# Top-k attention with channel mix: the weighted sums move behind the scores in PSUM, the ranks behind the exponentials, weighing stands after turning, the 1e-9 is added early

## The chip, the cores and the metric

The kernel runs on one core of one Trainium2 chip. The metric is the device time of one execution in microseconds (us); lower is better.

## What is computed

```python
# attention: B, H, S, D = 8, 8, 576, 64; top_k = 32
scores = scale * np.matmul(q, k.transpose(0, 1, 3, 2))
kth = np.partition(scores, -top_k, axis=-1)[..., -top_k:-top_k + 1]
scores = np.where(scores >= kth, scores, -1000000000.0)
attn = np.exp(scores - np.max(scores, axis=-1, keepdims=True))
attn = attn / (np.sum(attn, axis=-1, keepdims=True) + 1e-09)
x = np.matmul(attn, v)            # then (B, S, H * D)
# channel mix: d_model 512, d_ff 1024
xk = mu_k * x + (1.0 - mu_k) * x_prev
xr = mu_r * x + (1.0 - mu_r) * x_prev
k = np.maximum(xk @ w_k, 0.0)
out = 1.0 / (1.0 + np.exp(-(xr @ w_r))) * (k * k @ w_v)
```

All of it is float32, at full precision.

## The kernel before

The attention is cut into 288 tiles of 128 query rows by 576 keys. A visit is one pair of heads (`hp`) of one batch with either four tiles (`i` = 0 to 3) or five (`i` = 4 to 8; tile 8 holds the last 64 rows of both heads). Four tiles, or tile 8 alone, make a unit: there are 96 of them. `pipeline` runs a software pipeline: each turn of its `while` loop is one slot `n`, in which every stage works on another tile. Tile n is scored (`scores`, L230 and L234, TensorE) and copied out (`keep`, L239, ScalarE); tile n-1 gives candidates (`candidates`, L263, VectorE); tile n-2 is ranked, bounded and counted (`bounds` L274, `count` L279 on ScalarE, `below` L282 on GpSimd); tile n-3 gets its threshold from nine ranks (`threshold`, L287), its exponentials (`exps`, L290, ScalarE) and its mask with the row sums (`mask`, L293, VectorE); tile n-4 is turned (`turn_tile`, four transposes L309, two more at L319 for the last 64 columns of a pair of tiles) and copied out by ScalarE (L310, L320); for tile n-5, if its number is odd or 8, a pair of tiles is weighed with the values (`weigh`, L367 and L369: 16 matmuls and 4, 160 times in all). Once for each unit ScalarE adds 1e-9 to the row sums (`inverse`, L325), VectorE takes the reciprocal (`inverse2`, L329), GpSimd spreads it (`spread`, L334), TensorE turns it (`turn_inverse`, L340), ScalarE copies it out (L345, L349), and VectorE multiplies it onto the weighted sums (`place`, L374 to L379).

The order of these steps inside a slot is the list `ORDER` (L42); each engine runs its own instructions strictly in that order. Between them the class `Lanes` puts the work of the channel mix: matmuls (`mix`, L427 to L429) at the end of TensorE's slot, copies out of PSUM at `evac` and other ScalarE work at `act`, as far as a budget of planned costs (`PACE`, `SHARE`, `PIECE`) allows. The budget and the costs are the same before and after, so the same matmuls stand in the same slots.

PSUM has eight banks of 512 float32 values per partition. Two banks hold one tile of scores, with the nine `ranks` in the same two banks. Two more hold the exponentials of one tile (576 values, so 64 of them lie in the second bank), and behind them the weighted `sums`. The other four go round (`psM`) for everything that is turned or mixed. There is one buffer each of scores and of exponentials, and instructions of different engines that touch the same bank wait for each other, reads included. So before the change the weighing waits for this slot's exponentials (both lie in the same bank) and the mask for the weighing; the scores wait for `nine` (L287) of the slot before, which reads the ranks, and `nine` waits for `keep`.

Of the kernel before, what the change touches and what calls it, by code (L numbers as in the profile page):

```python
# [9 lines left out]
F32 = mybir.dt.float32  # L10
# [3 lines left out]
AF = mybir.ActivationFunctionType  # L14
OP = mybir.AluOpType
PSUM = bass.MemoryType.PSUM

B, H, S, D = 8, 8, 576, 64
# [3 lines left out]
HS = S // 2  # L22
# [16 lines left out]
PACE, SHARE, PIECE, CAP, MOST = 4.60, 0.74, 1.52, 4.45, 2  # L39
END, HASTE = 36, 1.20  # L40
EXPS, EVAC = 3, (0, 'et')
ORDER = """exp score weigh turn prep inv loads evac keep best0 c0 drop0 c1 best1 c2 drop1 first c3 best2 c4 bounds eighth count norm et high below act late c5 norm2 early thr c6 second place mix mask dve pool weights""".split()  # L42


@with_exitstack
def topk_attention_channel_mix(ctx: ExitStack, tc: tile.TileContext, q, k, v, mu_k, mu_r, w_k, w_v, w_r, out):
    nc = tc.nc
# [25 lines left out]
    def open_pools(stack, g, sfx):  # L73
        p = lambda n, bufs, **kw: stack.enter_context(tc.tile_pool(name=n + sfx, bufs=bufs, **kw))
        g.one = p("one", 1)
        g.two = p("two", 2)
        g.three = p("three", 3)
        g.four = p("four", 4)

        scored = p("psS", 1, space=PSUM).tile([128, 2 * 512], F32, name="ps")  # L80
        g.ps, g.ranks = scored[:, 512 - HS:512 + HS], scored[:, :9]


        g.se = p("psE", 1, space=PSUM).tile([128, 2 * 512], F32, name="se")
        g.pe = g.se[:, :S]
        g.sums = g.se[:, S:S + 256], g.se[:, S + 256:S + 320]
        nc.vector.tensor_copy(g.ranks, ranks_i)
        g.turns = 0
        g.ready = range(3 * HP + NFB) if sfx else []
        g.psM = g.psT = p("psM", 4, space=PSUM)  # L90
# [134 lines left out]
    def scores(g, P, i):  # L225
        hs = [slice(e * 64, (e + 1) * 64) for e in range(2)]
        if i < 2 * NKC:
            c, j = divmod(i - P.first, 2)
            for e, h in enumerate(hs):
                nc.tensor.matmul(g.ps[:, e * HS:(e + 1) * HS], lhsT=P.qs[j][h, c * 128:(c + 1) * 128], rhs=P.K[h, j], start=True, stop=True)  # L230
        else:
            for j in range(2):
                for e, h in enumerate(hs):
                    nc.tensor.matmul(g.ps[hs[j], e * HS:(e + 1) * HS], lhsT=P.qr[h, hs[j]], rhs=P.K[h, j], start=True, stop=True)  # L234
        return g.ps

    def keep(g, T):
        T.sc = g.four.tile([128, S], F32, name="sc")
        nc.scalar.activation(T.sc, T.ps, AF.Copy)  # L239

    def pick_exact(g, T):
        top = g.four.tile([128, TOPK], F32, name="top")
# [109 lines left out]
    def weigh(g, U, u):  # L352
        P = U.P
        if u == 0:
            U.pa = g.sums[U.u // 2]
        hs = [slice(j * 64, (j + 1) * 64) for j in range(2)]
        if U.u < 2:
            pa = U.pa[:, u * 128:(u + 1) * 128]
            ms = [[U.et[u, j][:, c, :] for j in range(2)] for c in range(NKC)]
            ls = [U.el[u][:, j * 128:(j + 1) * 128] for j in range(2)]  # L360
        else:
            pa = U.pa
            ms = [[U.et[0, 0][:, c, h] for h in hs] for c in range(NKC)]
            ls = [U.el[0][:, h] for h in hs]
        for c in range(NKC):
            for j in range(2):
                nc.tensor.matmul(pa[hs[j]], lhsT=P.v[:, j, c, :], rhs=ms[c][j], start=(c == 0), stop=False)  # L367
        for j in range(2):
            nc.tensor.matmul(pa[hs[j]], lhsT=P.vr[:, j], rhs=ls[j], start=False, stop=True)  # L369

    def place(U):
        xT, hp = U.xT, U.P.hp
        if U.u < 2 and U.P.near:
            nc.vector.tensor_mul(xT[:, hp, 1 + U.u * 256:1 + (U.u + 1) * 256], U.pa, U.ri)  # L374
        elif U.u < 2:
            x = xT[:, hp, 1:1 + MAIN].rearrange("p (q c) -> p c q", c=NKC)[:, 2 * U.u:2 * U.u + 2, :]
            nc.vector.tensor_mul(x, U.pa.rearrange("p (c q) -> p c q", c=2), U.ri.rearrange("p (c q) -> p c q", c=2))
        else:
            nc.vector.tensor_mul(xT[:, hp, 1 + MAIN:], U.pa, U.ri[:, :64])  # L379

# [186 lines left out]
    class Lanes:  # L567
# [9 lines left out]
        def at(self, slots, place, f, lane=None, cost=0.0):  # L577
            item = Env()
            item.f, item.lane, item.cost, item.done = f, lane, cost, False
            self.todo.setdefault((self.slot + slots, place), []).append(item)  # L580
            return item
# [16 lines left out]
        def run(self, place):  # L598
            for item in self.todo.pop((self.slot, place), []):
                self.do(item)  # L600
            while (item := self.first(self.queue.get(place, []))) and self.free[place] >= item.cost * SHARE:
                self.do(item)
                self.queue[place].remove(item)
# [79 lines left out]
    def new_batch(g):  # L683
        x = g.two.tile([128, HP, 1 + S], F32, name="xT")
        nc.gpsimd.memset(x[:, :, 0:1], 0.0)
        return x

    def pipeline(g):
# [91 lines left out]
        while n < total + 7 or "next" in state or L.busy():  # L780
# [21 lines left out]
            def score():  # L802
                if n < total:
                    P = Ps[p]
                    T = tiles[n] = Tile_()
                    T.n, T.i, T.P = n, i, P
                    if i == P.first:
                        if p % HP == 0:
                            state["seen"] = g.two.tile([128, HP, 3, 9], F32, name="seen")
                        P.group, P.seen = state["seen"], state["seen"][:, p % HP]  # L810
                    if i % 4 == 0:
                        U = units[p, i // 4] = Env()
                        U.u, U.P = i // 4, P
                        U.rs = g.four.tile([128, 4], F32, name="rs")
                    T.U = units[p, i // 4]
                    T.rs = T.U.rs[:, i % 4:i % 4 + 1]
                    T.ps = scores(g, P, i)
                    L.use("pe", 0.5)
# [23 lines left out]
            def weigh_():  # L842
                if W and (W.i % 2 or W.i == 8):
                    weigh(g, W.U, W.i // 2 % 2)
                    L.use("pe", 1.33 if W.i % 2 else 0.7)
# [31 lines left out]
            def ranks_(f, r):  # L877
                if C:
                    f(C, r)
# [15 lines left out]
            def keep_():  # L895
                if n < total:
                    keep(g, tiles[n])
                    L.use("act", 0.53)
# [43 lines left out]
            do.update({f"drop{r}": lambda r=r: ranks_(drop, r) for r in range(2)})  # L942
            for step in ORDER:
                if step in do:
# [7 lines left out]
    with ExitStack() as stack:  # L952
        g = Env()
        open_pools(stack, g, "")
        stack.enter_context(tc.manual_schedule())
        pipeline(g)
# [12 lines left out]
    with tc.If(again > 0):  # L969
        with tc.For_i(0, B, 1) as b, ExitStack() as stack:  # L970
            g = Env()
            open_pools(stack, g, "_again")
            L = Direct()
            xT = new_batch(g)
            rows = out[bass.ds(b, 1)].rearrange("o s d -> (o s) d")
            for hp in range(HP):
                P = Env()
                P.hp = hp
                prep_all(g, P, lambda x: x[bass.ds(b, 1)].rearrange("o h s d -> (o h) s d"), hp, L)
                for i in range(9):  # L980
                    T = Tile_()
                    T.i = i
                    if i % 4 == 0:
                        U = Env()
                        U.u, U.P, U.xT = i // 4, P, xT
                        U.rs = g.four.tile([128, 4], F32, name="rs")
                    T.U, T.rs = U, U.rs[:, i % 4:i % 4 + 1]
                    T.e = g.three.tile([128, S], F32, name="E")
                    T.ps = scores(g, P, i)
                    keep(g, T)  # L990
                    pick_exact(g, T)
                    T.nb = g.four.tile([128, 1], F32, name="nb")
                    nc.gpsimd.tensor_scalar(T.nb, T.max, -SCALE, 1.0, op0=OP.mult, op1=OP.mult)
                    exps(g, T)
                    mask(g, T)
                    g.px = None
                    turn_tile(g, T, L)
                    if i % 4 == 3 or i == 8:
                        inverse(g, U)
                        inverse2(U)  # L1000
                        spread(g, U)
                        g.px = None
                        turn_inverse(g, U, L)
                        for u in range(2 if i < 8 else 1):
                            weigh(g, U, u)
                        place(U)
# [26 lines left out]
```

## Time and profile before

| what | value |
|---|---|
| time, median of 3 runs (lowest to highest) | 1466.51 us (1463.87 to 1469.33) |
| profiled execution: its own time, its span | 1466.39 us, 1464.1 us |
| TensorE matmul (PE), weight load (PEld) busy | 1277.6 us (87%), 978.2 us (67%) |
| VectorE (DVE) busy | 1211.5 us (83%) |
| ScalarE (ACT) busy | 1170.4 us (80%) |
| GpSimd (POOL) busy | 970.5 us (66%) |
| chain that ended last, by engine | PE 57%, ACT 21%, DVE 15%, POOL 3% |

In the profile L12 is line 12 of the kernel, and `se<-et,v_in` means that the instruction writes `se` and reads `et` and `v_in`; `ps` are the scores, `se` the exponentials (and the sums behind them), `E` the masked exponentials, `pt` and `et` the turned ones before and after the copy, `sc` the kept scores, `sg` the signs, `rs` the row sums, `seen` the bounds and thresholds, `pk` and `pq` the turned keys and queries. A bracket with an arrow tells how long the engine had been idle before the instruction, and what released it. The four compute engines are all busy most of the time, so a wait matters where the engine that waits is the late one of its stretch. The first 300 us also hold the loading and splitting of the weights; the last 100 us hold only channel mix.

### The profile page before, as it was taken

How to read it: one execution, taken by the hardware profiler on the slowest of the kernel's cores; microseconds unless marked ns; L12 is line 12 of the kernel's file. 1: busy time of each engine (PE TensorE's matmuls, PEld its weight loads, DVE VectorE, ACT ScalarE, POOL GpSimd, SP SyncE). 2: the span in 40 equal slices, each digit the busy share in tenths (PEclk: the TensorE clock that was granted, in tenths of full speed). 3: DMA queues.
4: the chain of work that ended last, by engine and by line, in shares of the span. 5: the costliest groups of instructions: out<-in, count | busy, mean ns of one | idle time of the engine just before them, and what ended most of it. 6: DMA issues, size and time to landing. Idle time of an engine off the chain costs nothing.

```text
span 1464.1 us, 32963 instructions
## 1 busy us (share of the span) xinstructions
PE 1277.6 (87%) x9909; PEld 978.2 (67%) x9909; DVE 1211.5 (83%) x6454; ACT 1170.4 (80%) x2662; POOL 970.5 (66%) x876
## 2 busy tenths in 40 slices
PE   5665766899998999897989999999999898899997
PEld 3444554676776777585767676767767676677786
DVE  6778899887988989898988989898989898889610
ACT  5766777788888988887979888889998897888641
POOL 3656686567556856676767776767676765777673
PEclk9776787999999999999999999999999999999999
DMA  4332223211222122222121212222221222111000
GB/s 98 81 81 69 69 67 85 60 44 37 59 56 49 44 57 63 50 55 51 42 64 39 59 36 62 50 62 53 48 57 45 59 59 64 37 44 42 20 15 21
DMA packets 243817, 78.79 MB, mean 54 GB/s; under 512 B 236464, under 2 KB 236464, under 8 KB 243632
## 3 DMA queue, kind: packets, MB, share of 16 engines
q1 hardware_dynamic: 243632, 76.61, 21.8%
q8 instruction: 82, 1.34, 0.4%
q14 instruction: 103, 0.84, 0.2%
HBM read 67.11 MB, written 9.44 MB: 52 GB/s over the span
## 4 chain that ended last, share of the span: by engine, by line
PE 57%; ACT 21%; DVE 15%; POOL 3%; issue 2%; DMA 2%; SPq 0%; ACTq 0%; DVEq 0%; POOLq 0%
PE se L367 10%; PE pt L309 8%; PE ps L230 6%; PE ph L427 4%; PE ph L428 4%; PE ph L429 4%; ACT sg L279 4%; PE pv L429 3%; PE pv L427 3%; ACT se L290 3%; PE pv L428 3%; DVE cand L263 3%; ACT et L310 3%; ACT xm L403 3%; DVE E L293 2%; PE se L369 2%
## 5 line engine op out<-in xcount | busy, mean ns | idle before, releaser
L282 POOL TENSOR_TENSOR sg<-sc,sg 128x576 f32<-128x576 f32 x288 | 414.4, 1439 | 389.9 <-ACT sg L279 346.4
L263 DVE MAX8 cand<-sc 128x8 f32<-128x82 f32 (+1 forms) x2016 | 466.9, 232 | 1.5 <-ACT sc L239 0.9
L279 ACT ACTIVATE sg<-sc,seen 128x576 f32<-128x576 f32 x288 | 222.7, 773 | 64.9 <-DVE seen L274 60.7
L230 PE MATMUL ps<-K,qs 64*128 64x288 f32 x1024 | 207.2, 483 | 72.6 <-DVE nine L287 64.1
L239 ACT ACTIVATE sc<-ps 128x576 f32<-128x576 f32 x288 | 186.3, 647 | 81.3 <-PE ps L230 72.6
L367 PE MATMUL se<-et,v_in 128*64 128x128 f32 (+1 forms) x2560 | 184.1, 290 | 75.6 <-ACT se L290 70.3
L293 DVE SCALAR_TENSOR_TENSOR E<-sc,seen,se 128x576 f32<-128x576 f32 x288 | 232.5, 807 | 18.9 <-PE se L369 16.8
L367 PEld LDWEIGHTS se<-et,v_in 128*64 128x64 f32 x2560 | 144.1, 149 | 149.5 <-ACT se L290 129.8
L310 ACT ACTIVATE et<-pt 128x512 f32<-128x512 f32 x288 | 170.2, 591 | 72.6 <-PE pt L309 71.4
L290 ACT ACTIVATE se<-sc,seen 128x576 f32<-128x576 f32 x288 | 213.1, 740 | 8.5 <-DVE E L293 8.2
L909 DVE MAX8 top<-sg 128x8 f32<-128x576 f32 x288 | 216.1, 750 | 0.2 <-POOL sg L282 0.2
L309 PE MATMUL pt<-ident,E 128*128 128x128 f32 x1152 | 202.5, 302 | 1.2 <-DVE E L293 1.1
L309 PEld LDWEIGHTS pt<-ident,E 128*128 128x128 f32 x1152 | 130.1, 149 | 81.5 <-issue 37.3
L427 PE MATMUL ph<-xh,wk 128*128 128x256 f32 (+2 forms) x608 | 180.0, 296 | 2.6 <-ACT r L444 1.5
L428 PE MATMUL ph<-xl,wk 128*128 128x256 f32 (+2 forms) x608 | 172.2, 283 | 7.9 <-POOL xl L423 7.9
L230 PEld LDWEIGHTS ps<-K,qs 64*128 64x128 f32 x1024 | 82.5, 196 | 141.7 <-DVE nine L287 44.7
L266 DVE MAX8 top<-cand 128x8 f32<-128x56 f32 x864 | 176.5, 204 | 0.1
L429 PE MATMUL ph<-xh,wk 128*128 128x256 f32 (+2 forms) x608 | 171.0, 281 | 0.0
L427 PE MATMUL pv<-wv,hh 128*128 128x512 f32 (+1 forms) x296 | 125.6, 424 | 1.0 <-ACT et L310 1.0
L428 PEld LDWEIGHTS ph<-xl,wk 128*128 128x128 f32 x608 | 116.4, 191 | 10.3 <-POOL xl L423 10.2
L429 PE MATMUL pv<-wv,hl 128*128 128x512 f32 (+1 forms) x296 | 117.9, 398 | 2.8 <-POOL hl L448 2.7
L427 PEld LDWEIGHTS ph<-xh,wk 128*128 128x128 f32 x608 | 116.1, 191 | 5.5 <-ACT et L310 2.2
(99 smaller groups left out, 2878.9 us busy)
## 6 DMA issues: line engine op xcount, KB each, us to landing
kt<-in_k SPq DMA_DIRECT2D x256, 72.0 KB, 2.3
q_near<-in_q SPq DMA_DIRECT2D x256, 64.0 KB, 2.2
v_in<-in_v SPq DMA_DIRECT2D x128, 128.0 KB, 2.5
out<-eb SPq DMA_DIRECT2D x35, 256.0 KB, 2.1
wst<-in_moe_w_k SPq DMA_DIRECT2D x8, 512.0 KB, 4.1
wst<-in_moe_w_v SPq DMA_DIRECT2D x8, 512.0 KB, 3.7
vr_in<-in_v SPq DMA_DIRECT2D x64, 32.0 KB, 2.4
wst<-in_moe_w_r SPq DMA_DIRECT2D x4, 512.0 KB, 4.2
```

Of the source, the lines that this page charges most:

```text
L230: nc.tensor.matmul(g.ps[:, e * HS:(e + 1) * HS], lhsT=P.qs[j][h, c * 128:(c + 1) * 128], rhs=P.K[h, j], start=True, stop=True)
L263: nc.vector.max(T.cand[:, 8 * i:8 * i + 8], T.sc[:, CUTS[i]:CUTS[i + 1]])
L279: nc.scalar.activation(T.side, T.sc, AF.Sign, bias=T.under, scale=-BELOW, accum_out=T.cnt)
L282: nc.gpsimd.tensor_mul(T.side, T.sc, T.side)
L290: nc.scalar.activation(g.pe, T.sc, AF.Exp, bias=T.nb, scale=SCALE)
L293: nc.vector.scalar_tensor_tensor(T.e, T.sc, T.thr, g.pe, op0=OP.is_ge, op1=OP.mult, accum_out=T.rs)
L309: nc.tensor.transpose(pt[:, c, :], T.e[:, c * 128:(c + 1) * 128], ident)
L367: nc.tensor.matmul(pa[hs[j]], lhsT=P.v[:, j, c, :], rhs=ms[c][j], start=(c == 0), stop=False)
L427: nc.tensor.matmul(ps, lhsT=sh, rhs=mh, start=first, stop=False)
L428: nc.tensor.matmul(ps, lhsT=sh, rhs=ml, start=False, stop=False)
L429: nc.tensor.matmul(ps, lhsT=sl, rhs=mh, start=False, stop=last)
L909: nc.vector.max(M.top[:, 24:32], M.side)
```

## The change

The sums move from the banks of the exponentials into the two banks of the scores: each head's 288 scores now start at the beginning of a bank, and behind them lie 128 columns of sums in each bank, and 64 more for tile 8 in the first one. The ranks move from the scores' banks into the second bank of the exponentials. In the order, `weigh` goes from behind `score` to behind `keep`, and `norm` (L325) from behind `count` to behind `exp`. The remaining edits write the same operations with three-dimensional views. No instruction is added or taken away.

```diff
-ORDER = """exp score weigh turn prep inv loads evac keep best0 c0 drop0 ... bounds eighth count norm et high below act late c5 norm2 early thr c6 second place mix mask dve pool weights""".split()
+ORDER = """exp norm score turn prep inv loads evac keep weigh best0 c0 drop0 ... bounds eighth count et high below act late c5 norm2 early thr c6 second place mix mask dve pool weights""".split()
...
-        scored = p("psS", 1, space=PSUM).tile([128, 2 * 512], F32, name="ps")
-        g.ps, g.ranks = scored[:, 512 - HS:512 + HS], scored[:, :9]
-        g.se = p("psE", 1, space=PSUM).tile([128, 2 * 512], F32, name="se")
-        g.pe = g.se[:, :S]
-        g.sums = g.se[:, S:S + 256], g.se[:, S + 256:S + 320]
+        scored = p("psS", 1, space=PSUM).tile([128, 2, 512], F32, name="ps")
+        g.ps = scored[:, :, :HS]
+        g.sums = scored[:, :, HS:HS + 128], scored[:, 0, HS + 128:HS + 192]
+        se = p("psE", 1, space=PSUM).tile([128, 2 * 512], F32, name="se")
+        g.pe, g.ranks = se[:, :S], se[:, S:S + 9]
...
-                nc.tensor.matmul(g.ps[:, e * HS:(e + 1) * HS], lhsT=P.qs[j][h, c * 128:(c + 1) * 128], rhs=P.K[h, j], start=True, stop=True)
+                nc.tensor.matmul(g.ps[:, e], lhsT=P.qs[j][h, c * 128:(c + 1) * 128], rhs=P.K[h, j], start=True, stop=True)
...
-        nc.scalar.activation(T.sc, T.ps, AF.Copy)
+        nc.scalar.activation(T.sc.rearrange("p (e k) -> p e k", e=2), T.ps, AF.Copy)
...
-            pa = U.pa[:, u * 128:(u + 1) * 128]
+            pa = U.pa[:, u]
...
-            nc.vector.tensor_mul(xT[:, hp, 1 + U.u * 256:1 + (U.u + 1) * 256], U.pa, U.ri)
+            x = xT[:, hp, 1 + U.u * 256:1 + (U.u + 1) * 256].rearrange("p (u q) -> p u q", u=2)
+            nc.vector.tensor_mul(x, U.pa, U.ri.rearrange("p (u q) -> p u q", u=2))
```

TensorE in a slot that weighs, before: the scores (`ps<-K,qs`), the weighing (`se<-et,v_in`, `se<-el,vr_in`), the turning (`pt<-ident,E`), the last queries turned (`pr`), the reciprocals turned (`px<-ident,rb`).

```order
L230 MATMUL ps<-K,qs_6087 128x288 x2
L367 MATMUL se<-et_6078,v_in 64x128
L367 MATMUL se<-et_6134,v_in 64x128
...
L369 MATMUL se<-el_76,vr_in 64x128 x2
L309 MATMUL pt<-ident,E 128x128 x4
L199 MATMUL pr<-ident,qr_in 128x128
L340 MATMUL px<-ident,rb 128x128 x2
```

The same slot after the change:

```order
L230 MATMUL ps<-K,qs_6077 128x288 x2
L309 MATMUL pt<-ident,E 128x128 x4
L199 MATMUL pr<-ident,qr_in 128x128
L340 MATMUL px<-ident,rb 128x128 x2
L367 MATMUL ps<-et_6068,v_in 64x128
L367 MATMUL ps<-et_6135,v_in 64x128
...
L369 MATMUL ps<-el_76,vr_in 64x128 x2
```

The weighing has gone from between the scores and the turning to the end of the attention's work in the slot, directly ahead of the mix, and it now writes the banks of the scores.

ScalarE in a slot in which a unit ends, before: the exponentials, the copy of the scores, the count, the 1e-9 (`rs<-rs`), the copy of the turned tile.

```order
L290 ACTIVATE se<-sc,seen 128x576
L239 ACTIVATE sc<-ps 128x576
L279 ACTIVATE sg,cnt<-sc,seen 128x576
L325 ACTIVATE rs<-rs 128x4
L310 ACTIVATE et_14075<-pt 128x512
```

After:

```order
L290 ACTIVATE se<-sc,seen 128x576
L325 ACTIVATE rs<-rs 128x4
L239 ACTIVATE sc<-ps 128x576
L279 ACTIVATE sg,cnt<-sc,seen 128x576
L310 ACTIVATE et_14076<-pt 128x512
```

The small instruction with the 1e-9 stands two places earlier, ahead of the copy of the scores. VectorE, GpSimd and the DMA queue keep their order.

## Rows read from the trace of the kernel before

**Rows 1.** Busy time of the engines in two stretches, with PE's granted clock.
```profile
core 0: us, PE busy (x) PEld busy (x) DVE busy (x) ACT busy (x) POOL busy (x), PEclk, DMA share, GB/s
0.00:300.00 300.00, 201.16 (x1316) 144.75 (x1318) 245.87 (x1188) 208.97 (x458) 188.03 (x163) 0.81 0.31 74
300.00:1400.00 1100.00, 1022.22 (x8267) 788.27 (x8264) 958.05 (x5253) 942.40 (x2162) 750.64 (x677) 0.98 0.21 50
```
**Rows 2.** Waits of PE from 300 to 1400 us: total, times, longest.
```profile
PE se L367 <- ACT se L290: 51.2, 42, 2.4
PE ps L230 <- DVE nine L287: 9.0, 7, 2.1
```
**Rows 3.** Waits of DVE from 300 to 1400 us.
```profile
DVE rs L329 <- ACT rs L325: 68.4, 81, 3.1
DVE nine L287 <- ACT sc L239: 40.7, 63, 2.3
DVE E L293 <- PE se L369: 11.0, 11, 1.5
```
**Rows 4.** Waits of ACT from 300 to 1400 us.
```profile
ACT et L310 <- PE pt L309: 47.4, 95, 2.2
ACT sg L279 <- DVE seen L274: 17.5, 30, 1.7
```
**Rows 5.** Waits of DVE from 0 to 300 us.
```profile
DVE rs L329 <- ACT rs L325: 8.7, 15, 2.1
DVE E L293 <- PE se L369: 5.8, 11, 1.1
```
**Rows 6.** Matmuls of the weighing (L367) from 300 to 1400 us, 16 to each weighing.
```profile
300.00:1400.00 1100.00, 143.16 (x2154) 112.03 (x2150) 0.98 0.21 50
```
**Rows 7.** Timeline of a slot without a stall: start us, us, instruction.
```profile
581.54 1.09 PE L367 MATMUL se<-et,v_in 128*64 128x128 f32 x16
581.74 0.65 ACT L239 ACTIVATE sc<-ps 128x576 f32<-128x576 f32 x1 [1.21 <-PE ps L230]
...
582.42 0.23 DVE L287 SCALAR_TENSOR_TENSOR nine<-ps,cnt,top 128x9 f32<-128x9 f32 x1 [0.28 <-ACT sc L239]
...
582.78 0.66 PE L309 MATMUL pt<-ident,E 128*128 128x128 f32 x4
...
583.28 0.38 PE L199 MATMUL pq<-ident,q_near 128*128 128x128 f32 x2
...
583.42 0.47 PE L427 MATMUL pv<-wv,hh 128*128 128x512 f32 x1
```
**Rows 8.** Timeline of a slot with a stall.
```profile
595.35 1.12 PE L230 MATMUL ps<-K,qs 64*128 64x288 f32 x4 [1.46 <-DVE nine L287]
595.37 0.41 DVE L374 TENSOR_TENSOR xT<-se,ri 128x256 f32<-128x256 f32 x1
...
597.66 0.73 ACT L290 ACTIVATE se<-sc,seen 128x576 f32<-128x576 f32 x1
598.33 0.64 ACT L239 ACTIVATE sc<-ps 128x576 f32<-128x576 f32 x1
...
598.45 1.98 PE L367 MATMUL se<-et,v_in 128*64 128x128 f32 x16 [1.98 <-ACT se L290]
...
600.90 0.81 DVE L293 SCALAR_TENSOR_TENSOR E<-sc,seen,se 128x576 f32<-128x576 f32 x1 [1.51 <-PE se L369]
...
601.94 0.60 ACT L310 ACTIVATE et<-pt 128x512 f32<-128x512 f32 x1 [2.21 <-PE pt L309]
```
**Rows 9.** Timeline of ACT: the last idle time ahead of the first and last stalls.
```profile
301.35 0.60 ACT L310 ACTIVATE et<-pt 128x512 f32<-128x512 f32 x1 [0.33 <-PE pt L309]
...
383.26 0.78 ACT L279 ACTIVATE sg<-sc,seen 128x576 f32<-128x576 f32 x1 [1.67 <-DVE seen L274]
...
1296.08 0.60 ACT L310 ACTIVATE et<-pt 128x512 f32<-128x512 f32 x1 [0.31 <-PE pt L309]
...
1327.31 0.78 ACT L279 ACTIVATE sg<-sc,seen 128x576 f32<-128x576 f32 x1 [1.08 <-DVE seen L274]
```
**Rows 10.** DMA issues by line: KB each, us to landing.
```profile
kt<-in_k SPq DMA_DIRECT2D x256, 72.0 KB, 2.3
```

More of the change, by code (lines that the diff above doesn't have):

```diff
@@ L41 @@
 EXPS, EVAC = 3, (0, 'et')
-ORDER = """exp score weigh turn prep inv loads evac keep best0 c0 drop0 c1 best1 c2 drop1 first c3 best2 c4 bounds eighth count norm et high below act late c5 norm2 early thr c6 second place mix mask dve pool weights""".split()
+ORDER = """exp norm score turn prep inv loads evac keep weigh best0 c0 drop0 c1 best1 c2 drop1 first c3 best2 c4 bounds eighth count et high below act late c5 norm2 early thr c6 second place mix mask dve pool weights""".split()
 @with_exitstack
@@ L233, in scores @@
                 for e, h in enumerate(hs):
-                    nc.tensor.matmul(g.ps[hs[j], e * HS:(e + 1) * HS], lhsT=P.qr[h, hs[j]], rhs=P.K[h, j], start=True, stop=True)
+                    nc.tensor.matmul(g.ps[hs[j], e], lhsT=P.qr[h, hs[j]], rhs=P.K[h, j], start=True, stop=True)
         return g.ps
@@ L373, in place @@
         if U.u < 2 and U.P.near:
-            nc.vector.tensor_mul(xT[:, hp, 1 + U.u * 256:1 + (U.u + 1) * 256], U.pa, U.ri)
+            x = xT[:, hp, 1 + U.u * 256:1 + (U.u + 1) * 256].rearrange("p (u q) -> p u q", u=2)
+            nc.vector.tensor_mul(x, U.pa, U.ri.rearrange("p (u q) -> p u q", u=2))
         elif U.u < 2:
             x = xT[:, hp, 1:1 + MAIN].rearrange("p (q c) -> p c q", c=NKC)[:, 2 * U.u:2 * U.u + 2, :]
-            nc.vector.tensor_mul(x, U.pa.rearrange("p (c q) -> p c q", c=2), U.ri.rearrange("p (c q) -> p c q", c=2))
+            nc.vector.tensor_mul(x, U.pa, U.ri.rearrange("p (c q) -> p c q", c=2))
         else:
```

## The prediction

> **What bounds the kernel now.** I read the busy times by stretch first. From 300 to 1400 us TensorE (PE) is busy 1022.2 us of 1100, VectorE (DVE) 958.1 and ScalarE (ACT) 942.4 [rows 1]: PE is the late engine of most slots, with 77.8 us of idle time, and DVE has 141.9 us of it. In the first 300 us it is the other way round: DVE has 245.9 us of work, PE 201.2. So the sum is about PE's gaps after 300 us, and about DVE's before.
>
> Then the waits. PE's gaps from 300 to 1400 us are nearly all of one kind: 42 waits of the weighing for the exponentials, 51.2 us, and 9.0 us of the scores for the ranks' reader [rows 2]. They are there because the sums share a bank with the exponentials, and the ranks one with the scores; no number flows between them. DVE's gaps are three: the reciprocal for the 1e-9 (68.4 us), `nine` for the copy of the scores (40.7) and the mask for the weighing (11.0) [rows 3]. All five hang on the three things that the change moves: the sums, the ranks and the 1e-9.
>
> Last the timeline, of two slots. In a slot without a stall [rows 7] PE goes from scores to weighing (581.54), turning (582.78), queries (583.28) and mix (583.42) without a gap, while DVE waits for `keep` (ends 582.39) to run `nine` at 582.42: DVE is ahead and waits, which costs nothing. In a slot with a stall [rows 8] the exponentials end at 598.39, PE has stood 1.98 us and starts to weigh at 598.45; the mask then waits 1.51 us for the weighing, ACT waits 2.21 us for the turning behind it. Three engines stand in turn. The weighing also takes 1.98 us there and 1.09 in the other slot: PE stood still before it, and runs at 1.2 GHz.
>
> **The change part by part.** The sum is made against the profiled execution, 1466.4 us, which is the median of the runs (1466.5) to 0.1 us.
>
> *First 300 us.* DVE sets the pace, and two of its waits end: for the 1e-9 (8.7 us) and for the weighing (5.8) [rows 5]. At most 14.5 us come back, at least none, if the weights' copies are late instead. I take **-10**: DVE is nearest to being the only limit here.
>
> *The stalls of the weighing, 51.2 us.* It no longer waits for the exponentials, but for `keep`, which stands behind them on ACT: in the stalled slot 598.97 in place of 598.39 [rows 8], 0.58 us later. Against that PE now does the turning (0.50 us, from 582.78 to 583.28) and the queries (0.14) first [rows 7], and two transposes more of the reciprocals where a unit ends (as long as the queries': 0.14). So with ACT as late as now a stall gets shorter by 0.06 to 0.20 us, or more where three key transposes stand there, and longer by some 0.6 where a copy at `evac` stands between exponentials and `keep`. For 42 stalls I take **-8**, between -16 and +10.
>
> *A new wait where there was none.* The window holds 2154 matmuls of the weighing [rows 6], so 135 weighings, 93 of them without a stall. In such a slot PE would be ready to weigh at 581.54 + 0.50 + 0.14 = 582.18, and `keep` ends at 582.39, to which the start adds 0.06 (as 598.39 to 598.45 in rows 8): 0.27 us lost, and nothing where keys and reciprocals fill the time. This is lost on the late engine. 93 x 0.15 = **+14**, between 0 and +25.
>
> *ACT earlier.* Why are the exponentials late? I followed ACT back from each stall to its last idle time. In 21 of 42, the first and the last of them at 301.35 and 1296.08 [rows 9], it had worked without a pause since a copy of a turned tile that waited for PE, some 0.33 us. The turning now stands ahead of the weighing, 1.24 us earlier (581.54 to 582.78 in rows 7), and most of the 47.4 us that these copies wait [rows 4] goes: 21 x 0.33 = **-7**, between 0 and -15.
>
> *DVE earlier.* In 10 of 42, the first and last at 383.26 and 1327.31 [rows 9], the last idle time was a wait for DVE's bounds, up to 1.67 us. DVE now waits for `keep` no longer at `nine` and for the 1e-9 no longer in mid-slot; the 109.1 us of these two [rows 3] let it run further ahead before the next short slots. 10 x 0.8 = **-8**, between 0 and -17. The 9.0 us of the scores go in two of three slots, since after a unit `place` reads the scores' banks now, and in the stalled slot it ends at 595.78, later than `nine` did (scores at 595.35) [rows 8]: **-6**, between 0 and -9.
>
> *The clock.* The mean granted clock of 0.98 [rows 1] means that 4% of the 1100 us ran at 1.2 GHz, at most 22 us of extra time. Fewer long stalls give back a part: **-4**, between 0 and -15.
>
> *At nothing:* the 1e-9 ahead of `keep` puts a small ACT instruction into 96 slots, where ACT waits for the scores (1.21 us in rows 7); if that cover goes, it delays `keep` by its own short time. Ranks, views and banks change no length. In the queue of the DMAs the loads of values wait for a visit's last weighing, and loads of queries and keys queue behind; the weighing that needs the values moves as far as the one they wait for. Keys land 2.3 us after the issue [rows 10] and are used at the next slot's turning; in two short slots that could be late, with PE waiting for keys in place of exponentials.
>
> Sum: -10 - 8 + 14 - 7 - 8 - 6 - 4 = -29 us, so **1437 us** (2.0% faster).
>
> **The rivals.** *(a) One wait for another.* By the direct terms alone, stalls and new waits, the middle gets 6 us slower; if ACT and DVE do not get ahead, half of the first stretch (5) and of the scores' wait (3) is all that pays: 1466 - 5 - 3 + 6 = 1464, with 1457 to 1474 around it. For it: in 21 stalls the chain lies on ACT alone, whose work is the same. Against it: rows 8 show DVE and ACT idle because of the weighing, and they no longer would be. The Trainium skill ("PSUM — Partial Sum Buffer", section on bank collisions) tells that any two engines at one bank and the same partitions must be kept apart, two reads included. The trace agrees: `nine` waits 40.7 us for a copy that also only reads. By that rule alone the change swaps partners (weighing with `keep`, `place` with the scores) and the outcome would be this case.
>
> *(b) Slower.* The new wait stands in every weighing, at the spot where PE is late, with all the mix of the slot behind it. If ACT comes to `keep` later than the scores end also in the slots without a stall, since copies at `evac` stand ahead of it, 0.27 us becomes up to 0.8: 93 x 0.30 = 28 us in place of 14, the stalls get longer (+5 in place of -8), ACT and the clock gain nothing, DVE half: 1466 + 28 + 5 - 10 - 4 - 6 = 1479, with 1475 to 1495 around it. It decides from the point at which the wait for `keep` passes 0.3 us on the mean of all weighings. Against it: in rows 7 ACT waits 1.21 us for the scores, so it is early there.
>
> *(c) Much faster.* With its partners gone DVE runs up to most of a slot ahead, and short slots no longer catch it late: two thirds of the 51.2 us, of the 22 us of the clock and all 14.5 us at the start would come back: 1466 - 34 - 15 - 15 - 9 + 14 = 1407, with 1385 to 1420 around it. Against it: ACT, at 942 us, has little room.
>
> **How the numbers follow.** A measurement of this kernel tells about 0.5% from no change, so faster is below 1459.1 us and slower above 1473.8. The forecast, 1420 to 1456, has 0.56; (c) 0.10; (a) 0.19, of which 0.03 lie below 1459; (b) 0.15. Faster 0.69, same 0.16, slower 0.15. The range from 1412 to 1474 takes in the forecast, (a) and the upper half of (c); (b) and the rest of (c), 0.20, are left out.
>
> **What would show it.** In the profile after, PE's waits before the weighing should name the copy of the scores (L239), with more than 100 of them short, some 0.2 us, and 40 to 50 us in all; waits for the exponentials there must be gone, and so must the reciprocal's and the mask's on DVE. Copies of turned tiles should hardly wait. DVE and ACT should show new idle time elsewhere, at the candidates for `keep`. I am wrong if PE's idle time between 300 and 1300 us is not smaller; if the waits for L239 pass 60 us, (b) is at work; if they stay under 25, (c).

## The result and the profile after

The changed kernel takes 1451.45 us (median, 1449.69 to 1453.04) against 1466.01 us before in the same runs: ratio 0.9898, interval 0.9876 to 0.9921. It is faster by 1.0%, inside the range, and gains half of what was forecast. The profiled execution has a span of 1450.3 us.

The busy times by stretch, after (same columns as [rows 1]):

```profile
0.00:300.00 300.00, 210.87 (x1367) 147.26 (x1368) 266.22 (x1232) 216.31 (x476) 195.89 (x167) 0.82 0.31 76
300.00:1400.00 1100.00, 1038.78 (x8266) 788.22 (x8265) 933.50 (x5213) 931.94 (x2154) 749.45 (x682) 0.99 0.21 50
```

In the first 300 us VectorE (DVE) now gets 266 us of its work done where it got 246. From 300 to 1400 us TensorE (PE) looks busier, by 16.6 us. Neither tells yet where the time went, since the same microsecond holds another tile in the two runs. Better is to cut by tiles: the scores of tile 72 start at 396.26 us before and at 380.48 after, those of the last tile, 287, at 1361.35 and 1348.90. So 15.8 us are gained by tile 72, and from there on 3.3 us are lost again. The stretch between these two tiles, before:

```profile
396.26:1361.35 965.09, 898.99 (x7297) 690.98 (x7296) 859.35 (x4748) 838.14 (x1923) 660.89 (x593) 0.98 0.22 52
```

and after:

```profile
380.48:1348.90 968.42, 914.39 (x7296) 692.10 (x7296) 844.36 (x4756) 832.10 (x1925) 655.57 (x592) 0.98 0.22 52
```

PE runs the same matmuls at the same granted clock, and its busy time is 15.4 us longer. That is no more work; what it is comes below, with the order alone.

PE's waits from 300 to 1400 us, after (total, times, longest), against [rows 2]:

```profile
PE ps L367 <- ACT sc L239: 23.7, 29, 2.0
PE ps L230 <- DVE xT L375: 18.4, 7, 5.6
...
PE ps L230 <- DVE xT L380: 2.6, 2, 1.6
```

The weighing now waits for the copy of the scores, and the scores wait for `place` (L375) where they waited for `nine`. DVE's waits in the same stretch, against [rows 3]:

```profile
DVE xT L375 <- PE ps L369: 46.6, 27, 3.0
...
DVE xT L375 <- POOL xT L686: 16.3, 5, 4.0
DVE xT L375 <- ACT sc L239: 13.2, 17, 1.1
DVE nine L287 <- ACT se L290: 7.5, 16, 1.0
DVE rs L329 <- ACT rs L325: 5.8, 7, 2.4
```

Of the three old waits (68.4, 40.7 and 11.0 us) 5.8 us are left, as forecast, but `place` alone waits 76.1 us now: for the weighing of tile 8, which writes the same banks in its slot, for the copy of the scores, and for a memset on GpSimd (L686). ScalarE (ACT), against [rows 4]:

```profile
ACT sc L239 <- PE ps L230: 89.0, 105, 2.7
ACT se L290 <- DVE E L293: 19.6, 34, 2.9
```

The copies of turned tiles, which waited 47.4 us, hardly wait any more; ACT waits for the scores instead (60.7 us before).

### The profile page after: what moved, and what is told of

Read it like the earlier page. It is cut to its first block, busy times and chain, and to the rows that moved or that the text cites. A ratio compares the mean times of both kernels' runs of the same rounds, so it can differ in the third digit from the quotient of the medians.

```text
span 1450.3 us, 32922 instructions
## 1 busy us (share of the span) xinstructions
PE 1291.7 (89%) x9909; PEld 971.8 (67%) x9909; DVE 1205.3 (83%) x6454; ACT 1162.3 (80%) x2662; POOL 967.6 (67%) x876
## 4 chain that ended last, share of the span: by engine, by line
PE 57%; DVE 16%; ACT 16%; POOL 5%; issue 3%; DMA 1%; SPq 1%; ACTq 0%; DVEq 0%; POOLq 0%
PE ps L367 8%; PE ps L230 7%; PE pt L309 6%; PE ph L428 5%; PE ph L429 4%; PE ph L430 4%; PE pv L428 4%; PE pv L430 4%; PE pv L429 3%; DVE cand L263 3%; ACT sg L279 3%; ACT sc L239 3%; DVE E L293 2%; ACT xm L404 2%; ACT et L310 2%
## 5 line engine op out<-in xcount | busy, mean ns | idle before, releaser
L282 POOL TENSOR_TENSOR sg<-sc,sg 128x576 f32<-128x576 f32 x288 | 419.1, 1455 | 413.1 <-ACT sg L279 359.9
L239 ACT ACTIVATE sc<-ps 128x576 f32<-128x576 f32 x288 | 186.6, 648 | 126.9 <-PE ps L230 104.3
L290 ACT ACTIVATE se<-sc,seen 128x576 f32<-128x576 f32 x288 | 213.9, 743 | 24.0 <-DVE E L293 23.7
L309 PEld LDWEIGHTS pt<-ident,E 128*128 128x128 f32 x1152 | 127.1, 146 | 156.7 <-issue 99.8
L309 PE MATMUL pt<-ident,E 128*128 128x128 f32 x1152 | 197.6, 296 | 35.6 <-DVE E L293 32.0
L367 PE MATMUL ps<-et,v_in 128*64 128x128 f32 (+1 forms) x2560 | 178.4, 286 | 28.7 <-ACT sc L239 27.8
L367 PEld LDWEIGHTS ps<-et,v_in 128*64 128x64 f32 x2560 | 140.1, 147 | 61.0 <-ACT sc L239 52.8
```

The source lines that it names most:

```text
L239: nc.scalar.activation(T.sc.rearrange("p (e k) -> p e k", e=2), T.ps, AF.Copy)
L282: nc.gpsimd.tensor_mul(T.side, T.sc, T.side)
L309: nc.tensor.transpose(pt[:, c, :], T.e[:, c * 128:(c + 1) * 128], ident)
```

## The experiments

Each time stands as ratio to the kernel before, measured beside it. Where the text speaks of tiles, the start of their scores was read in the profiled executions; relative to the kernel before, in us. Each column is one execution, which can lie off the median of its kernel: by -3.7 us for the 1e-9 alone, -3.0 for the PSUM places alone, -2.8 for the memset in single columns, under 2 for the others.

| kernel | tile 60 | tile 72 | tile 180 | tile 287 |
|---|---|---|---|---|
| the change | -9.5 | -15.8 | -14.7 | -12.4 |
| 1e-9 early alone | -2.4 | -6.9 | -10.6 | -10.8 |
| order alone | -3.0 | -9.1 | -14.4 | -15.4 |
| both moves of the order, PSUM as before | -6.8 | -10.5 | -16.4 | -18.5 |
| PSUM places alone | -3.9 | -8.5 | +8.6 | +13.2 |
| the change, weighing behind the mix | -12.2 | -17.4 | -23.1 | -31.3 |
| the change, memset in single columns | -13.1 | -19.4 | -25.0 | -26.4 |
| weighing behind the mix, xT made ready earlier | -12.5 | -17.7 | -31.6 | -44.7 |

### The parts one by one

**The 1e-9 early, alone.**

```diff
-ORDER = """exp score weigh turn ... eighth count norm et ...
+ORDER = """exp norm score weigh turn ... eighth count et ...
```

> The kernel before with one part of the change: the 1e-9 (L325) early, all else as before. The changed kernel gained its 15 us in the first 72 tiles and nothing after. Theory A (the middle of the change was eaten by the weighing's new wait for keep, the first stretch gained because VectorE and ScalarE no longer wait): the reciprocal's wait (77 us in all, 15 of them in the first 72 tiles) nearly goes, the first stretch gets 4 to 8 us shorter, the middle, where PE is late, 0 to 3: 1456 to 1463 us, ratio 0.993 to 0.998. Rival B (VectorE's wait for the 1e-9 costs nothing anywhere): 1466, ratio 0.999 to 1.001.

Measured: 1458.65 us, 0.9953 (0.9935 to 0.9972). A holds: 8 us. The profiled execution, which is 3.7 us faster than the median, gains 6.9 us by tile 72 and 10.8 by tile 287. In the middle the wait of the reciprocal went from 68.4 us to 7.1, and another took its place on DVE (300 to 1400 us):

```profile
DVE nine L287 <- ACT sc L239: 81.1, 124, 2.0
...
DVE rs L329 <- ACT rs L325: 7.1, 9, 3.2
```

40.7 us had become 81.1: there DVE is ahead of PE, and a wait taken away from it is paid at the next one.

**The ranks behind the exponentials, alone.**

```diff
-        g.ps, g.ranks = scored[:, 512 - HS:512 + HS], scored[:, :9]
+        g.ps = scored[:, 512 - HS:512 + HS]
...
+        g.ranks = g.se[:, S + 320:S + 329]
         nc.vector.tensor_copy(g.ranks, ranks_i)
```

> The kernel before with one part of the change: the ranks behind the exponentials and the sums, all else as before; the scores no longer wait for nine (L287), nine waits for the exponentials in place of keep. Theory A: the weighing still waits for the exponentials and the mask for the weighing, so little comes of it: 0 to -4 us, ratio 0.997 to 1.000. Rival B (the 56 us that PE waits for nine in the first 72 tiles were the gain): 8 to 14 us faster, ratio 0.990 to 0.995.

Measured: 1467.11 us, 1.0003 (0.9991 to 1.0015). Nothing, as A said. PE's 55 us of waits for `nine` in the first 300 us became waits for the exponentials (line numbers one higher in this kernel):

```profile
PE se L368 <- ACT se L291: 48.6, 17, 4.9
```

**The order alone: weighing behind the copy of the scores, PSUM as before.**

```diff
-ORDER = """exp score weigh turn prep inv loads evac keep best0 ...
+ORDER = """exp score turn prep inv loads evac keep weigh best0 ...
```

> The kernel before with one part of the change: the order alone, weighing behind keep and so behind the turning; the sums stay behind the exponentials. The weighing waits for exponentials that ended long before, so PE's short waits for keep are not there, but the mask waits for a weighing that ends about 1 us later in 160 slots. Theory A: PE gains some 20 of the 46 us that it loses between scores and weighing, the copies of the turned tiles no longer wait, the mask loses part of it: -15 to 0 us, ratio 0.990 to 1.000. Rival B (the mask's wait decides): 5 to 20 us slower, ratio 1.003 to 1.014.

Measured: 1452.64 us, 0.9904 (0.9889 to 0.992). A holds near its better end: this one word in a list gives what the whole change gives. PE's waits before the weighing fell from 51.2 us to 12.5, and the mask paid on DVE, where there was room (300 to 1400 us):

```profile
PE se L367 <- ACT se L290: 12.5, 22, 1.3
DVE E L293 <- PE se L369: 49.2, 70, 1.5
```

This run also tells what the weighing's new place in PE's queue costs by itself. The stretch from tile 72 to tile 287 here:

```profile
387.17:1345.91 958.74, 912.17 (x7297) 689.56 (x7296) 848.52 (x4747) 837.06 (x1924) 662.56 (x592) 0.99 0.22 52
```

PE's busy time is 13.2 us above that of the kernel before, nearly as in the change, although the weighing does not wait for `keep` here. Tile 114 shows why. Before (the slot of [rows 7], whose scores start at 580.86), it takes 4.13 us to the next scores:

```profile
584.99 0.76 PE L230 MATMUL ps<-K,qs 64*128 64x288 f32 x4
```

With the order alone it takes 4.33 us, and the weighing waits for nothing (the exponentials have ended 1.4 us earlier):

```profile
570.95 0.76 PE L230 MATMUL ps<-K,qs 64*128 64x288 f32 x4
571.64 0.66 PE L309 MATMUL pt<-ident,E 128*128 128x128 f32 x4
572.13 0.38 PE L199 MATMUL pq<-ident,q_near 128*128 128x128 f32 x2
572.44 1.09 PE L367 MATMUL se<-et,v_in 128*64 128x128 f32 x16
...
575.28 0.76 PE L230 MATMUL ps<-K,qs 64*128 64x288 f32 x4
```

The granted clock is 1.00 in both slots. From the queries to the next matmul pass 0.31 us here, where 0.14 us passed before, and the last four matmuls of the weighing (L369) start 0.31 us ahead of what follows them in both. So a weighing between the transposes and the mix costs some 0.2 us without any wait.

**Both moves of the order, PSUM as before.** 

```diff
-ORDER = """exp score weigh turn prep inv loads evac keep best0 ... count norm et ...
+ORDER = """exp norm score turn prep inv loads evac keep weigh best0 ... count et ...
```

> The kernel before with both moves of the order (weighing behind keep, 1e-9 early) and PSUM laid out as before. Alone they gave 13.8 and 7.8 us. Theory A (the order gives the gain of the change, the new PSUM places give nothing or take some back in the middle): the two add up at least in part, 16 to 24 us, 1442 to 1450 us, ratio 0.984 to 0.989, so faster than the whole change. Rival B (both moves cure the same lateness, and the sums' new place is needed for the rest): 12 to 15 us, ratio 0.990 to 0.992, no faster than the change.

Measured: 1448.34 us, 0.9878 (0.986 to 0.9896). By its time A: 17.2 us of the 21.5 that the parts gave, so they overlap a little. The interval overlaps the change's own, so that it is faster than the change is not shown; that the new PSUM places add nothing that can be measured to the order, as the change stands, is.

**The PSUM places alone, with the order of before.**

```diff
-ORDER = """exp norm score turn prep inv loads evac keep weigh best0 ... count et ...
+ORDER = """exp score weigh turn prep inv loads evac keep best0 ... count norm et ...
```

> The changed kernel's PSUM places (sums behind the scores, ranks behind the exponentials) with the order of before: weighing directly behind the scores, 1e-9 late. Theory A: the copy of the scores now waits for the weighing, 1.3 us in each of 160 slots, on ScalarE, and the turning stays behind the weighing: 5 to 40 us slower than before, ratio 1.003 to 1.027. Rival B (parting the weighing from exponentials and mask is worth it by itself): 5 to 15 us faster than before, ratio 0.990 to 0.997.

Measured: 1481.98 us, 1.0107 (1.0088 to 1.0126), 16 us slower, as A said. The copy of the scores waits for a weighing that stands ahead of it in its banks (ACT, 300 to 1400 us):

```profile
ACT sc L239 <- PE ps L369: 123.7, 94, 3.5
```

### What holds the middle

**The weighing behind the mix.** The planned cost stays where it was, so the mix keeps its slots.

```diff
-... keep weigh best0 ... second place mix mask ...
+... keep weigh best0 ... second place mix weighing mask ...
...
             def weigh_():
                 if W and (W.i % 2 or W.i == 8):
-                    weigh(g, W.U, W.i // 2 % 2)
                     L.use("pe", 1.33 if W.i % 2 else 0.7)
+            def weighing():
+                if W and (W.i % 2 or W.i == 8):
+                    weigh(g, W.U, W.i // 2 % 2)
...
```

> The changed kernel with the weighing's instructions behind the slot's mix, planned costs unchanged: keep has ended long before, so the weighing's wait for it (42 us in the slots from tile 72 on, short ones included) must go, and place no longer waits for the weighing of tile 8 in its own slot. Theory A (the wait for keep ate the gain of the middle): 15 to 35 us faster than the changed kernel, 1417 to 1437 us, ratio 0.967 to 0.981. Rival B (place holds the middle: the scores wait for it and it waits for the memset of xT): 0 to 6 us faster than the changed kernel, ratio 0.986 to 0.990. Rival C (ScalarE and PE have no more to give, the idle time only moves): within 4 us of the changed kernel, PE's idle time shows at another line.

Measured: 1434.82 us, 0.9793 (0.978 to 0.9807), 16.6 us faster than the change: A, at its lower end. From tile 72 to 287 it gains 13.9 us where the change lost 3.4. It takes away two things at once, the wait for `keep` and the place between the transposes and the mix, and does not part them: tile 114 (scores at 563.48) takes 4.14 us again, as before the change, and the busy time from tile 72 to 287 is 898.8 us again.

```profile
564.66 0.38 PE L199 MATMUL pq<-ident,q_near 128*128 128x128 f32 x2
564.79 0.48 PE L428 MATMUL pv<-wv,hh 128*128 128x512 f32 x1
...
567.62 0.76 PE L230 MATMUL ps<-K,qs 64*128 64x288 f32 x4
```

What is left of waits on PE (300 to 1400 us):

```profile
PE ps L230 <- DVE xT L375: 17.8, 6, 5.6
PE ps L367 <- ACT sc L239: 9.5, 8, 1.7
```

**`place` of tiles 4 to 7 one slot later.**

```diff
-            U.ri = g.one.tile([128, 256], F32, name="ri")
+            U.ri = g.two.tile([128, 256], F32, name="ri")
...
-                T = tiles.get(n - 6)
-                if T and ends(T):
+                for T in (tiles.get(n - 7), tiles.get(n - 6)):
+                    if not T or not ends(T) or T.n != n - (7 if T.i == 7 else 6):
+                        continue
...
```

> The changed kernel with the placing of the unit of tiles 4 to 7 one slot later (and two buffers of reciprocals for it), so that it no longer waits for the weighing of tile 8, which writes the same banks in its slot (46.6 us on VectorE from 300 to 1400 us). Theory A (VectorE is not late there; the wait for keep on PE is what holds the middle): within 4 us of the changed kernel, ratio to before 0.987 to 0.992. Rival B (place's wait on VectorE holds the middle): 6 to 14 us faster than the changed kernel, ratio 0.980 to 0.986.

Measured: 1450.83 us, 0.9897 (0.9879 to 0.9915): the change's own time. The longest wait on DVE, 46.6 us, was gone and brought nothing. A holds as far as DVE goes: it is not late there.

**xT made ready two slots earlier**, first on the kernel with the late weighing:

```diff
+                if V and ends(V) and V.P.b not in xT:
+                    b = V.P.b
+                    if state["start"] < (b - 1) * S:
+                        save()
...
+                    if b > 1:
+                        L.force(g.read)
+                    xT[b] = new_batch(g)
                 T = tiles.get(n - 6)
                 if T and ends(T):
                     U = T.U
-                    if U.P.b not in xT:
-                        if state["start"] < (U.P.b - 1) * S:
-                            save()
-                        if U.P.b > 1:
-                            L.force(g.read)
-                        xT[U.P.b] = new_batch(g)
```

> The kernel with the weighing behind the mix, and in it the new batch's xT made ready two slots earlier (forced reads of the old one and the memset on GpSimd). In that kernel PE still waits 17.8 us in 6 places for scores that wait for place, which waits for the memset, up to 5.6 us each. Theory A (these are pure loss at the six batch starts of the middle): 6 to 15 us faster than the kernel with the weighing behind the mix, 1420 to 1429 us, ratio 0.968 to 0.975. Rival B (the work forced early delays GpSimd and ScalarE as much): within 4 us of it, ratio 0.976 to 0.982.

Measured: 1420.14 us, 0.968 (0.9665 to 0.9695), 14.7 us less than with the late weighing alone, as A said. The scores' wait for `place` fell from 17.8 us to 5.3:

```profile
PE ps L230 <- DVE xT L375: 5.3, 4, 2.0
```

This is the fastest of all, 3.2% below the kernel before.

**The same on the changed kernel itself.**

```diff
+                if V and ends(V) and V.P.b not in xT:
...
+                    xT[b] = new_batch(g)
                 T = tiles.get(n - 6)
```

> The changed kernel, with the new batch's xT made ready two slots earlier and nothing else. PE waited there 18.4 us in 7 places for scores behind place, nearly all of it where place waited for the memset. Theory A (that wait is the second thing that ate the gain of the middle, apart from the wait for keep): 8 to 16 us faster than the changed kernel, 1435 to 1443 us, ratio 0.979 to 0.985. Rival B (only the wait for keep ate it; in the kernel with the late weighing the memset mattered because that wait was gone): within 4 us of the changed kernel, ratio 0.987 to 0.992.

Measured: 1441.18 us, 0.9825 (0.9809 to 0.9841), 10 us faster than the change. A holds by the time: the wait of `place` costs the change that much, with the wait for the copy of the scores still there. The forced reads moved with the memset; the next experiment parts them.

**The memset of xT's first column in single columns.** The waits written into the program tell why `place` waits for the memset at all. Before, no placing waits for GpSimd. After the change the first of each of the eight batches does (and one more, which keeps its wait here). The output of `place` is now a view of two runs of 128; the memset writes four elements, 577 apart. They share no element, and a wait was put between them all the same.

```diff
-        nc.gpsimd.memset(x[:, :, 0:1], 0.0)
+        for h in range(HP):
+            nc.gpsimd.memset(x[:, h, 0:1], 0.0)
```

> The changed kernel with the one memset of xT's first column (four elements, 577 apart) written as four memsets of one element. In the kernel before, place has no wait for GpSimd; in the changed one its first unit of each batch has, since its output is now a view of two runs, and such a view and a strided memset are taken to overlap though they share no element. With single columns that wait is gone from the program. Theory A (this wait, made by the view, is what the earlier xT cured): 8 to 14 us faster than the changed kernel, 1437 to 1444 us, ratio 0.979 to 0.985, no wait of place for the memset. Rival B (the forced reads on GpSimd matter, which only the earlier xT moved): within 4 us of the changed kernel, ratio 0.987 to 0.992.

Measured: 1441.14 us, 0.9825 (0.9811 to 0.9838): A, to 0.04 us the time of the experiment before. Its interval lies clear below that of both moves of the order with PSUM as before (0.986 to 0.9896): without this wait the new places are worth something, some 7 us. The scores' wait for `place` (300 to 1400 us) is then

```profile
PE ps L230 <- DVE xT L375: 5.9, 5, 2.0
```

where the change has 18.4 us. The episode in the timeline of the changed kernel that it cures:

```profile
581.13 2.31 POOL L409 TENSOR_TENSOR xm<-xm,xT 128x512 f32<-128x512 f32 x2 [0.33 <-ACT xm L404]
583.38 0.10 POOL L686 MEMSET xT<- 128x4 f32 x1
583.52 0.42 DVE L375 TENSOR_TENSOR xT<-ps,ri 128x256 f32<-128x256 f32 x1 [3.98 <-POOL xT L686]
...
584.00 1.33 PE L230 MATMUL ps<-K,qs 64*128 64x288 f32 x4 [5.62 <-DVE xT L375]
...
585.26 1.11 PE L309 MATMUL pt<-ident,E 128*128 128x128 f32 x4
```

The memset takes 0.10 us, but stands behind 2.3 us of other work in GpSimd's queue; DVE waits for it, and since the sums now lie in the scores' banks, PE waits for DVE: 5.62 us, after which scores and turning run at 1.2 GHz (granted clock 0.50 from 582 to 588 us; 1.33 and 1.11 us, against 0.76 and 0.66 in a slot without a stall).

### Two bounds

**The late weighing with PSUM as before** (behind the mask, since both use the exponentials' banks).

```diff
-ORDER = """exp score weigh turn ... count norm et ... second place mix mask dve ...
+ORDER = """exp norm score weigh turn ... count et ... second place mix mask weighing dve ...
...
```

> The 1e-9 early and the weighing behind the mix, but the sums and ranks in the PSUM places of before (the weighing stands behind the mask, too, since both use the exponentials' banks). The weighing now waits for the mask of its slot and the next slot's exponentials for the weighing, which ends the slot on PE. Theory A (the sums' new place pays only together with a late weighing: it lets the exponentials and the mask run beside it): slower than the kernel with the weighing behind the mix and the new places by 10 to 60 us, 1445 to 1495 us, ratio 0.986 to 1.020. Rival B (the new places are worth nothing in any order): within 5 us of that kernel, ratio 0.976 to 0.983.

Measured: 1464.84 us, 0.999 (0.9977 to 1.0002). A: 30 us slower than with the new places. The exponentials of the next slot wait for the weighing (ACT, 300 to 1400 us):

```profile
ACT se L290 <- PE se L369: 76.2, 94, 2.4
```

So the new places do pay, where the order lets them.

**The wait for the copy of the scores laid bare.**

```diff
-... score turn prep inv loads evac keep weigh best0 ...
+... score evac keep weigh turn prep inv loads best0 ...
```

> The changed kernel with the turning behind the weighing again: PE goes from the scores straight to the weighing, so the wait for keep stands bare, some 0.9 us after the end of the scores in each of 160 slots in place of some 0.3 us. Theory A (this wait is paid by PE in full in most slots of the middle): 40 to 100 us slower than the changed kernel, 1490 to 1550 us, ratio 1.017 to 1.058. Rival B (PE has slack and the wait is hidden): within 10 us of the changed kernel, ratio 0.984 to 0.998.

Measured: 1596.55 us, 1.089 (1.0871 to 1.0908), 145 us slower than the change, well past A's upper end. The wait does stand bare, and the waits fit a ring that I had not counted: the turning stands behind it, ACT's copies of turned tiles behind that, and the next copy of the scores behind them. No run takes the ring apart. PE's waits (300 to 1400 us):

```profile
PE ps L367 <- ACT sc L239: 141.4, 122, 3.8
```

and ACT's:

```profile
ACT et L310 <- PE pt L309: 154.5, 121, 2.8
```

## Why the prediction was right, and where it was not

The time lies in the range, at half of the forecast gain. That it does is partly luck: errors of 10 us and more on single terms stand against each other.

**The first stretch.** Forecast -10 us up to 300 us; measured -9.5 at tile 60 (336 us before). The size holds. By tile 72 it is 15.8 us, and the forecast had missed a source. DVE's waits up to tile 72, before:

```profile
DVE wmag L126 <- ACT wmag L122: 24.3, 18, 2.5
DVE rs L329 <- ACT rs L325: 15.4, 22, 3.1
DVE E L293 <- PE se L369: 8.6, 14, 1.5
```

and after:

```profile
DVE wmag L126 <- ACT wmag L122: 9.7, 18, 2.1
```

The weights' magnitudes (L122), which ACT makes for DVE, come 14.6 us less late, all of it in the first 300 us, beside the two waits that I had counted. The order of the weighing brings this: up to 385 us the wait for them is 4.3 us with the order alone and 24.8 with the 1e-9 alone. ACT's waits for turned tiles, 29.6 us before, are gone with the order alone, which may be the reason; but they are gone with the PSUM places alone too, where the wait for the magnitudes is 20.0 us, so this stays open. I had named exactly these copies as what might come last instead, and they were helped too.

**The stalls and the new wait, +6 us together.** The size held, what it is made of did not. In the 119 slots from tile 72 to 286 that weigh, PE spent 128.4 us before from the start of the scores to the start of the weighing; with 0.69 us for the scores that is 46.3 us of waiting. After, the time from the last preparing transposes to the weighing is 62.3 us where 19.9 us passed from them to the next matmul before, so 42.4 us; with 3.4 us between scores and turning, 45.8 us. One loss took the place of another, as in rival (a), but not all of the 42.4 us is a wait for `keep`. In 71 of the 119 slots the weighing starts 0.05 us after the copy has ended; in most of the others it stands 0.17 us behind a transpose of keys or 0.20 behind one of queries or reciprocals, just as in the run with the order alone, where it does not wait for the copy. Counted from this spacing, all 119 lose 26 us to the wait. The other 16 us are the price of the new place, which my sum did not have: I took 0.14 us from the queries to the weighing, and it is 0.31 without a wait. Both show in tile 114 of the change, which takes 4.42 us to the next scores (566.05 to 570.47), beside 4.33 with the order alone and 4.13 before:

```profile
566.05 0.76 PE L230 MATMUL ps<-K,qs 64*128 64x288 f32 x4
566.73 0.66 PE L309 MATMUL pt<-ident,E 128*128 128x128 f32 x4
566.93 0.65 ACT L239 ACTIVATE sc<-ps 128x576 f32<-128x576 f32 x1 [0.73 <-PE ps L230]
567.23 0.38 PE L199 MATMUL pq<-ident,q_near 128*128 128x128 f32 x2
...
567.63 1.09 PE L367 MATMUL ps<-et,v_in 128*64 128x128 f32 x16
...
570.47 0.76 PE L230 MATMUL ps<-K,qs 64*128 64x288 f32 x4
```

From the queries to the weighing pass 0.40 us, where 0.14 us passed to the next matmul in [rows 7]: 0.26 us, against 0.27 forecast, of which 0.17 us are the place and 0.09 the wait. So the profile's list, 23.7 us for L239, misses little, and my test, less than 25 us of these waits means much faster, was a wrong test: it had nothing in it for a loss that is no wait. Moving the weighing behind the mix takes away the place's cost and most of the wait, 42.4 us by this count, yet only 17.3 us of the middle came back; 9.5 us of the wait are left, and where the rest went is open.

**ACT and DVE earlier, -7 and -8 us.** Little of it came in the middle: taking 46.6 us of waits from DVE (`place` one slot later) moved nothing, and the 1e-9 alone gave 3.9 us between tiles 72 and 287 of its profiled execution. In the middle PE sets the pace, and a wait of DVE counts as far as PE comes to wait for it. No run measures the -7 for ACT by itself.

**The scores' wait, -6 us, and the views at nothing: this step failed.** I wrote that ranks, views and banks change no length. That is so, but the view of `place` brought a wait for a memset, and the sums' place handed it on to PE: the scores' wait for DVE went from 9.0 us to 21.0. Without the memset's wait it is 8.5 us and the time 1441.1 us. The wait cost 10 us, by the two experiments that remove it.

**The clock, -4 us.** The granted clock is 0.98 before and after between tiles 72 and 287, so next to nothing came back.

**Luck.** Without the memset's wait the time is 4 us from the forecast, but not because the other terms held. In the profiled execution of that kernel 19.4 us are gained by tile 72, where 10 were forecast for the start, and 7.0 from there to tile 287, where the terms for the middle (-8, +14, -7, -8, -6, -4) add up to -19. The two errors nearly cancel.

**Rival (b)** needed the wait for `keep` to pass 0.3 us on the mean of all weighings; it is 26/119 = 0.22 us, so its condition did not come about. It looked only at the new wait; what decides is this and the place's 16 us against the old wait of 46.3/119 = 0.39 us.

**The rule on PSUM banks** (the Trainium skill, "PSUM — Partial Sum Buffer", bank collisions) tells that engines at one bank have to be kept apart. The traces agree: with each change of places waits appear between new partners in a bank, as the copy of the scores waits 123.7 us for the weighing with the PSUM places alone. Rival (a), the swap of partners, gave the middle +6 - 3 = +3 us, and it was 3.3 us longer; (a) as a whole, 1464 us, did not come true, since the start gained 15.8 us and not 5.

## What to carry to other kernels

Sharing a PSUM bank ties two instructions together; choose partners whose use of it is far apart in time, and then move the work in the queue so that the partner has long ended. Here the new PSUM place was worth nothing with the weighing directly behind the copy that it waits for (1451 us against 1448 for the old places; some 7 us better without the memset's wait), and 30 us with the weighing at the end of the slot (1435 us against 1465 for the old places). Compare the same slot from scores to scores in two kernels: a place in the queue can cost time without a wait. Ask of each wait taken away which engine is late in that stretch, and compare program order for waits that a new view brings: one such wait cost 10 us of a gain of 25.

## What was not expected of the hardware

A place in TensorE's queue can have a price without any wait, and the profile counts it as busy time. In its rows the scores, the weighing, and the transposes with the mix have three shapes: `64*128`, `128*64` and `128*128`. At a granted clock of 1.00, 0.14 us pass from the start of the two queries' transposes to the mix, of the same shape, and 0.31 us to the weighing, of another; from the last four matmuls of the weighing to the turning or the mix it is again 0.31 or 0.32 us. Before, a slot that weighs and mixes had three changes of shape; with the weighing between the transposes and the mix it has four, and with the weighing behind the mix three again. Tile 114 follows this: 4.13, 4.33 (order alone, no wait) and 4.14 us, and so does the busy time from tile 72 to 287: 899.0, 912.2 and 898.8 us. That the change of shape is the reason was not tested by itself.
